# Strided attention and a Strassen MLP on one core: loads held for q instead of x, two more batches transposed by DMA, steps dealt anew

## The chip, the core and the metric

The kernel runs on one core of one Trainium2 chip. The core has five engines: TensorE (PE; its weight loads appear as PEld), VectorE (DVE), ScalarE (ACT), GpSimd (POOL) and SyncE (SP). Each works through its own list of instructions in order, and waits where an operand is not there yet. Transfers are issued by GpSimd and SyncE and carried out by 16 DMA engines. The metric is the time of one execution in microseconds; before, the median of three runs was 282.69 us (282.55 to 283.13).

## The reference

Attention over 8 batches of 8 heads (576 positions of 64), then an MLP over the 4608 tokens. Heads 0 to 3 see a local window of 32 positions, heads 4 to 7 the earlier positions with the same remainder modulo 32:

```python
rel = pos[:, None] - pos[None, :]
mask_local = (rel >= 0) & (rel < 32)
mask_strided = (rel >= 0) & (pos[None, :] % 32 == pos[:, None] % 32)
scores = np.where(masks, q @ k.T / 8, -1e9)       # masks: local for h < 4, else strided
attn = softmax(scores) @ v                        # [8, 8, 576, 64]
x = attn.transpose(0, 2, 1, 3).reshape(4608, 512)
h = x @ w_in                                      # 512 x 2048
out = (h * np.tanh(softplus(h))) @ w_out          # 2048 x 512
```

## The kernel before

Inputs are float32; GpSimd's DMAs cast them to bf16 while they load. Products are bf16 with float32 sums.

*Attention.* A batch is loaded as six tiles: `ks`, `qs` (strided k and q), `kl`, `ql` (local), `vraw` and `vl` (v for the two kinds). k and q must be transposed so that the 64 elements of a head lie along the partitions. For batches 0 to 2 TensorE transposes them, from batch 3 on four DMA transposes do, which SyncE issues: `kTs`, `qTs`, `kTl`, `qTl` (`transpose_by_dma`, L189). There is one buffer of each, so the loads of the next batch may only start once the tiles have been read. Scores, exponential (ScalarE), mask (VectorE), the product with v (L299), and the division by the sum (`norm`, L311 and L316) give `x_l` and `x_s`, the attention of the local and the strided heads, with positions on the partitions.

*From x to xT.* The MLP needs x with its 512 channels on the partitions: `xT`, a ring of four batches, 128 channels by four, where channels 0 and 1 are the local heads and 2 and 3 the strided ones. The local ones go by two DMA transposes from batch 2 on (`xt_dma`, L323). The strided ones of batches 0 to 5 are transposed by TensorE (`xt`, L346), two groups of eight matmuls a batch, each followed by a copy into `xT`. Those of batches 6 and 7 are transposed by one DMA into `ks` (`xs_dma`, L329), which is free then, and copied to `xT` in two pieces (`xs_copy`).

*MLP.* The tokens are nine blocks of 512, `t` = 0 to 8. For each, `x @ w_in`, mish (ScalarE writes `gT`), and `@ w_out`. Each product is a Strassen-Winograd product: seven products of halves instead of eight, for which VectorE makes sums of x (`xs`), of g (`gs`), of the weights (`wis`, `wos`), and of the results (`hh`, `ee`, `osb`). TensorE writes into eight PSUM banks (`set`, `ee`, `at`). Two stores of a block are issued by SyncE (L567).

*The order of the work.* Nothing is scheduled automatically. Every instruction stands where the table `PLANS` puts it: ten strings, one for each block and a last one for the rest. A function `do` reads a string word by word and emits each step's instructions to their engines. Plan `t` holds the MLP of block `t` and mostly the attention of batch `t + 1`; `^` and `_` ahead of a word mean the next or the previous `t`, `@3` names the batch. Of the words, `ld` is a load, `D:ks` a DMA transpose of k or q, `T` and `t` their transposes by TensorE and the copy, `q`, `e`, `k`, `v`, `r` scores, exponential, mask, product with v and division, `y` the two DMA transposes of local x, `X` and `xc` the transposes of strided x by TensorE and the copy, `V` and `vc` the same by DMA, `x` a sum of x, `g` and `n` sums of g, a figure the product of that number of the first layer, `m` with a figure one of the second, `st` a store. The letter behind a last colon is the engine (`D` VectorE, `A` ScalarE) or the bank.

*Holds.* GpSimd would issue loads as early as buffers allow. At seven places the table has `hold`: a copy of two elements on GpSimd out of the tile that some DMA transpose writes. GpSimd waits there until that transfer has landed, and the loads behind it on GpSimd start only then:

```python
elif f == "hold":
    e = (b % RING) * S + S - 1
    src = {"ks": kTs, "qs": qTs, "kl": kTl, "ql": qTl}[x[0]][0:1, 0:2] if x else xT[0:1, 0:2, e]
    Po.tensor_copy(hold[0:1, 0:2], src)
```

With no argument it reads `xT` (the landing of the transposed local x of batch `b`), with `qs` it reads `qTs`. Six holds of the kernel before are of the first kind, one, for the loads of batch 5, is of the second.

Of the kernel before, what the change touches and what calls it, by code (L numbers as in the profile page):

```python
# [19 lines left out]
SU = 80  # L20
CS, PN = 8, 72
# [24 lines left out]
def kernel(ctx, tc, q, k, v, moe_w_in, moe_w_out, out):  # L46
    nc = tc.nc
    B, H, S, D = q.shape
# [45 lines left out]
    x_s = sb([128, CS * 4, D], "x_s")  # L94

# [129 lines left out]
    class Attn:  # L225
# [102 lines left out]
        def xs_dma(self):  # L328
            nc.sync.dma_start_transpose(  # L329
                flat(ks)[:, 0:16 * SU].rearrange("c (u n) -> c u n", u=16),  # L330
                x_s[0:SU].rearrange("p u d -> p (u d)"),
            )

        def xs_copy(self, hf, eng):
            t0 = (self.b % RING) * S
            cast(
                eng, xT[:, 2 + hf, t0:t0 + S].rearrange("p (n j) -> p n j", j=CS),
                flat(ks)[:, 8 * SU * hf:8 * SU * hf + 8 * SU].rearrange("p (j n) -> p n j", j=CS)[:, 0:PN, :],
            )
# [229 lines left out]
    with tc.manual_schedule():  # L569
# [158 lines left out]
        def go(plan, t=0):  # L728
            for w in plan.split():
# [27 lines left out]
            ),  # L757
            (
# [6 lines left out]
            ),  # L765
            (
# [10 lines left out]
            ),  # L777
            (
# [8 lines left out]
            ),  # L787
            (
# [39 lines left out]
            ),  # L828
            (
                "m1:1 m1c:1:D _3:3 _E:3 m1c:0:D m5:0 m5:1 _4:3 g:1 m6:0 g:2 m6:1 _Z:3 m2:0 m5c:A m6c:1:D m7:1 m6c:0:A "  # L830
                "m7c:1 g:3 m2:1 z:b:A w:b:S m3:1 m7:0 m7c:0 m3:0 m3c m4:1 m4:0 z:0:A z:1:A st:1 w:0:S w:1:A "
            ),
        )
        for t, plan in enumerate(PLANS):
# [32 lines left out]
```

## Time and profile before

| | |
|---|---|
| median of three runs | 282.69 us (282.55 to 283.13) |
| the profiled execution | 283.62 us |
| its span, first to last instruction | 281.9 us |
| matmuls / weight loads in the program | 3235 recorded / 3241 |
| moved by DMA | 37.35 MB in 98242 packets |
| of the 16 DMA engines' time, loads on GpSimd's queue | 65.3% of the span |
| transposes and stores on SyncE's queue | 28.5% of the span |

The span is what the profile covers; the execution's own time is longer by what lies around it. The digits of the page are the busy share in tenths of 40 slices, each 281.9 / 40 = 7.05 us long. A timeline row is start, length, engine, line, operation, written and read tile, and in brackets the idle time before it with what ended that. Rows with a `q` behind the engine (SPq, POOLq) are issues of DMAs: their length is not the transfer's, which ends later with its landing. The profile after has lines shifted by one, since a line is added near the top.

### The profile page before, as it was taken

How to read it: one execution, taken by the hardware profiler on the slowest of the kernel's cores; microseconds unless marked ns; L12 is line 12 of the kernel's file. 1: busy time of each engine (PE TensorE's matmuls, PEld its weight loads, DVE VectorE, ACT ScalarE, POOL GpSimd, SP SyncE). 2: the span in 40 equal slices, each digit the busy share in tenths (PEclk: the TensorE clock that was granted, in tenths of full speed). 3: DMA queues.
4: the chain of work that ended last, by engine and by line, in shares of the span. 5: the costliest groups of instructions: out<-in, count | busy, mean ns of one | idle time of the engine just before them, and what ended most of it. 6: DMA issues, size and time to landing. Idle time of an engine off the chain costs nothing.

```text
span 281.9 us, 7629 instructions
## 1 busy us (share of the span) xinstructions
PE 273.2 (97%) x3235; PEld 226.5 (80%) x3241; DVE 225.5 (80%) x384; ACT 186.1 (66%) x288; POOL 57.6 (20%) x78
## 2 busy tenths in 40 slices
PE   8998999999999999999999999998999999999994
PEld 3657746678989888888898989886989888888883
DVE  3789878999899895999689969888889966837761
ACT  2577974799776797479757986687488217624830
POOL 8543421440027007200540027000100000000000
PEclk9999999999999999999999999999999999999999
DMA  7999999999929998999799989989644003002104
GB/s 142 191 207 203 205 189 197 146 222 92 168 46 141 120 168 169 193 112 155 203 147 100 137 228 145 116 146 155 161 136 96 10 2 149 2 3 98 53 0 149
DMA packets 98242, 37.35 MB, mean 133 GB/s; under 512 B 79800, under 2 KB 93688, under 8 KB 98208
## 3 DMA queue, kind: packets, MB, share of 16 engines
q0 software_dynamic: 57808, 18.30, 65.3%
q1 hardware_dynamic: 40112, 18.32, 28.5%
q8 instruction: 25, 0.41, 0.6%
q10 hardware_dynamic: 288, 0.25, 0.4%
q14 instruction: 9, 0.07, 0.1%
HBM read 37.05 MB, written 9.44 MB: 165 GB/s over the span
## 4 chain that ended last, share of the span: by engine, by line
PE 90%; DVE 3%; DMA 2%; ACT 2%; issue 1%; SPq 1%; DVEq 0%; ACTq 0%
PE set L121 52%; PE ee L121 21%; PE at L121 9%; PE at L299 4%; DMA qTs<-qs 2%; SPq L189 1%; PE at L346 1%; PE ee L346 1%; PE ee L202 1%; PE set L299 1%; DVE xs L115 1%; PE ee L208 0%; PE at L208 0%; DVE osb L112 0%; DVE wos L115 0%
## 5 line engine op out<-in xcount | busy, mean ns | idle before, releaser
L121 PEld LDWEIGHTS <-wis 128*128 128x128 bf16 x577 | 55.9, 99 | 10.4 <-issue 2.2
L121 PEld LDWEIGHTS <-gs 128*128 128x128 bf16 x512 | 48.9, 98 | 6.9 <-issue 0.5
L121 PEld LDWEIGHTS <-gT 128*128 128x128 bf16 x448 | 42.2, 98 | 9.4
L121 PEld LDWEIGHTS <-w_in 128*128 128x128 bf16 x436 | 40.8, 97 | 7.7 <-issue 1.2
L121 PE MATMUL set<-w_out,gT 128*128 128x256 bf16 (+1 forms) x299 | 46.1, 294 | 0.2
L121 PE MATMUL set<-xT,w_in 128*128 128x256 bf16 (+1 forms) x263 | 40.1, 275 | 1.0 <-ACT gT L450 0.8
L450 ACT ACTIVATE gT<-set 128x1024 bf16<-128x1024 f32 x32 | 32.8, 1024 | 8.8 <-PE set L121 7.2
L121 PE MATMUL set<-xs,wis 128*128 128x256 bf16 x256 | 38.4, 273 | 0.0
L110 ACT COPY set<-set 128x512 f32<-128x512 f32 x35 | 20.2, 576 | 16.0 <-PE set L121 14.8
L121 PE MATMUL set<-wos,gs 128*128 128x256 bf16 x224 | 28.0, 273 | 0.0
L115 DVE TENSOR_TENSOR hh<-set,hh 128x512 f32<-128x512 f32 x32 | 21.9, 685 | 5.4 <-PE set L121 5.1
L115 DVE TENSOR_TENSOR ee<-set,hh 128x512 f32<-128x512 f32 x32 | 22.3, 697 | 3.9 <-PE set L121 1.7
L448 ACT ACTIVATE gT<-hh 128x512 bf16<-128x512 f32 x35 | 22.0, 635 | 4.0 <-DVE hh L115 3.7
L686 POOL COPY hold<-xT 1x2 bf16<-1x2 bf16 x6 | 1.9, 317 | 106.3 <-DMA xT<-x_l 106.3
L115 DVE TENSOR_TENSOR gs<-gT,gs 128x2048 bf16<-128x2048 bf16 x16 | 19.5, 1221 | 3.6 <-ACT gT L448 1.8
L446 ACT ACTIVATE gT<-ee 128x512 bf16<-128x512 f32 x35 | 20.1, 595 | 2.0 <-PE ee L121 2.0
L121 PE MATMUL ee<-xs,wis 128*128 128x256 bf16 x140 | 20.8, 272 | 0.0
L121 PE MATMUL ee<-xT,wis 128*128 128x256 bf16 x140 | 20.8, 273 | 0.0
L110 ACT COPY hh<-ee 128x512 f32<-128x512 f32 x20 | 11.7, 585 | 12.5 <-PE ee L121 12.4
L115 DVE TENSOR_TENSOR gs<-gT 128x2048 bf16<-128x2048 bf16 x16 | 19.5, 1217 | 0.2 <-ACT gT L448 0.2
L316 DVE TENSOR_TENSOR x_s<-at,rden 72x768 bf16<-72x768 f32 (+1 forms) x22 | 18.8, 856 | 0.8
L121 PE MATMUL set<-xs,w_in 128*128 128x256 bf16 x128 | 19.2, 272 | 0.0
(145 smaller groups left out, 467.9 us busy)
## 6 DMA issues: line engine op xcount, KB each, us to landing
out_dram<-osb SPq DMA_DIRECT2D x17, 512.0 KB, 3.7
vl<-in_v_dram POOLq DMA_DIRECT2D x8, 288.0 KB, 12.3
w_out<-in_moe_w_out_dram POOLq DMA_DIRECT2D x4, 512.0 KB, 16.0
ks<-in_k_dram POOLq DMA_DIRECT2D x7, 288.0 KB, 11.6
qs<-in_q_dram POOLq DMA_DIRECT2D x7, 288.0 KB, 10.0
vraw<-in_v_dram POOLq DMA_DIRECT2D x7, 288.0 KB, 7.5
w_in<-in_moe_w_in_dram POOLq DMA_DIRECT2D x3, 512.0 KB, 14.6
kl<-in_k_dram POOLq DMA_DIRECT2D x10, 144.0 KB, 8.9
```

The source lines that it names most:

```text
L110: Sc.copy(out_, in_)
L115: eng.tensor_tensor(out=out_, in0=a, in1=b, op=op)
L121: PE.matmul(o, lhsT=lhsT, rhs=rhs, start=start, stop=stop, skip_group_check=True)
L189: nc.sync.dma_start_transpose(dst[:, 0:k * r].rearrange("c (u n) -> c u n", u=k), src[0:r].rearrange("p h x -> p (h x)" if n[1] == "s" els ...
L202: PE.transpose(tr[:, PN * u:PN * u + PN], src[0:PN, h, 128 * jj:128 * jj + 128], ident[0:PN, 0:PN])
L299: PE.matmul(po[:, e, i, :] if kind == "l" and self.apart else po[:, (n - n0) // per, (n - n0) % per, :], lhsT=pt[0:r, c0:c0 + 128], rhs=rh ...
L316: Dv.tensor_tensor(out=xo, in0=po[0:m, :, :, 0:D], in1=rd.unsqueeze(3).to_broadcast([m, nb, per, D]), op=ALU.mult,)
L346: PE.transpose(tr[:, n * j:n * j + n], x[0:n, u:u + 2, :].rearrange("p u d -> p (u d)"), ident[0:n, 0:n],)
L446: Sc.activation(o[:, 0:2, 256:512], two(E), AF.Mish)
L448: Sc.activation(o[:, 2:4, 256:512], two(h[:, 1, :]), AF.Mish)
L450: Sc.activation(o[:, :, 0:256].rearrange("p (b u) n -> p b u n", b=2), pair[:, 0:2, :].rearrange("p b (u n) -> p b u n", u=2), AF.Mish,)
L686: Po.tensor_copy(hold[0:1, 0:2], src)
```

## The change

Three edits. First, the DMA transpose of strided x gets a buffer of its own, `xst`, instead of `ks`. Second, the strided x of batches 4 and 5, too, is transposed by DMA (`V`, `vc`) and no longer by TensorE (`X`, `xc`). Third, the table is written anew: most steps stay near where they were but not where they stood, and two holds, those ahead of the strided q of batches 6 and 7, read `qTs` instead of `xT`.

```diff
@@ -92,6 +92,7 @@
     x_s = sb([128, CS * 4, D], "x_s")
+    xst = sb([128, 16 * SU], "xst")
@@ -327,7 +328,7 @@
         def xs_dma(self):
             nc.sync.dma_start_transpose(
-                flat(ks)[:, 0:16 * SU].rearrange("c (u n) -> c u n", u=16),
+                xst[:].rearrange("c (u n) -> c u n", u=16),
                 x_s[0:SU].rearrange("p u d -> p (u d)"),
             )
@@ -335,7 +336,7 @@
             cast(
                 eng, xT[:, 2 + hf, t0:t0 + S].rearrange("p (n j) -> p n j", j=CS),
-                flat(ks)[:, 8 * SU * hf:8 * SU * hf + 8 * SU].rearrange("p (j n) -> p n j", j=CS)[:, 0:PN, :],
+                xst[:, 8 * SU * hf:8 * SU * hf + 8 * SU].rearrange("p (j n) -> p n j", j=CS)[:, 0:PN, :],
             )
@@ -732,103 +733,103 @@
         PLANS = (
...
-                "7c:0 3:0 E:0 v:s0:A 6c:1 y:1 hold 4:0 st:1 k:s2:D 7:1 Z:0 r:s0:A 5:2 3:1 ld:vs@5 1:2 1c:2:A 7c:1 4:1 "
...
-                "7:2 7c:2 2:3 st:0 6:3 5c:3:A 6c:3 X:0:a 4:2 3:2 xc:0:a:D H:1 H:2 7:3 3:3 7c:3 ld:ks@6 Z:2 ^m1:0 E:2 n "
...
+                "hold:qs@5 st:1 ld:vs@5 ld:qs@6 H:3 "
...
+                "g:1 m5:0 g:2 _Z:3 ae q:l1:F q:l0:A m2:1 m6:1 m6:0 m6c:D e:l1:F g:3 e:l0:A k:l0:D _V q:l2:A e:l2:A "
...
```

What the table does to the order is seen engine by engine. GpSimd, from the hold behind the loads of batch 5 on to that behind the loads of batch 6; before:

```order
49 L686 COPY hold<-xT 1x2
50 L157 DMA vraw<-in_v_dram 72x4x512
51 L133 DMA qs<-in_q_dram 72x4x512
52 L151 DMA kl<-in_k_dram 96x12x64 x2
53 L151 DMA ql<-in_q_dram 96x12x64 x2
54 L133 DMA ks<-in_k_dram 72x4x512
55 L160 DMA vl_79<-in_v_dram 96x24x64
56 L686 COPY hold<-xT 1x2
```

The same place in the changed kernel:

```order
49 L687 COPY hold<-qTs 1x2
50 L158 DMA vraw<-in_v_dram 72x4x512
51 L134 DMA qs<-in_q_dram 72x4x512
52 L152 DMA kl<-in_k_dram 96x12x64 x2
53 L152 DMA ql<-in_q_dram 96x12x64 x2
54 L134 DMA ks<-in_k_dram 72x4x512
55 L161 DMA vl_79<-in_v_dram 96x24x64
56 L687 COPY hold<-qTs 1x2
```

The order is the same; rows 49 and 56 read another tile. SyncE, from the transpose of the strided q of batch 5 to the transposes of batch 6; before:

```order
18 L189 DMA_TRANSPOSE qTs<-qs 128x16x80
19 L323 DMA_TRANSPOSE xT<-x_l 128x6x96 x2
20 L567 DMA out_dram<-osb 128x2x512 x2
21 L189 DMA_TRANSPOSE kTs<-ks 128x16x80
22 L189 DMA_TRANSPOSE qTl<-ql 128x12x96
```

Changed:

```order
18 L190 DMA_TRANSPOSE qTs<-qs 128x16x80
19 L324 DMA_TRANSPOSE xT<-x_l 128x6x96 x2
20 L568 DMA out_dram<-osb 128x2x512
21 L330 DMA_TRANSPOSE xst<-x_s 128x16x80
22 L568 DMA out_dram<-osb 128x2x512
23 L190 DMA_TRANSPOSE kTs<-ks 128x16x80
24 L190 DMA_TRANSPOSE qTl<-ql 128x12x96
```

A transpose of x_s (of batch 4 here, and of batch 5 one round on) has come between the two stores. VectorE, where the attention of batch 2 is divided by its sums (`rden`) into `x_l`; before:

```order
118 L112 COPY set_102<-set_102 128x512
119 L311 RECIPROCAL rden<-at 96x2x6
120 L316 TENSOR_TENSOR x_l<-at,rden 96x768
121 L115 TENSOR_TENSOR gs<-gT,gs 128x2048
122 L311 RECIPROCAL rden<-at 96x2x6
123 L316 TENSOR_TENSOR x_l<-at,rden 96x768
```

Changed:

```order
118 L312 RECIPROCAL rden<-at 96x2x6
119 L317 TENSOR_TENSOR x_l<-at,rden 96x768
120 L113 COPY set_103<-set_103 128x512
121 L312 RECIPROCAL rden<-at 96x2x6
122 L317 TENSOR_TENSOR x_l<-at,rden 96x768
123 L116 TENSOR_TENSOR gs<-gT,gs 128x2048
```

The second `x_l` row now stands ahead of the `gs` sum instead of behind it. In all, TensorE has 3209 matmuls and weight loads instead of 3241, VectorE 369 rows instead of 377, ScalarE 297 instead of 289.

More of the change, by code (lines that the diff above doesn't have):

```diff
@@ L734 @@
                 "ld:ks@0 ld:qs@0 ld:vs@0 clear:1 clear:0 kc:D un:1:a un:1:a un:1:a un:1:a un:1:a un:1:a un:1:a un:1:a "
[22 rows of a table removed]
-            ),
-            (
[6 rows of a table removed]
-            ),
-            (
[10 rows of a table removed]
-            ),
-            (
[8 rows of a table removed]
-            ),
-            (
[8 rows of a table removed]
-            ),
-            (
[7 rows of a table removed]
-            ),
-            (
[7 rows of a table removed]
-            ),
-            (
[5 rows of a table removed]
-            ),
-            (
[4 rows of a table removed]
-            ),
-            (
-                "m1:1 m1c:1:D _3:3 _E:3 m1c:0:D m5:0 m5:1 _4:3 g:1 m6:0 g:2 m6:1 _Z:3 m2:0 m5c:A m6c:1:D m7:1 m6c:0:A "
-                "m7c:1 g:3 m2:1 z:b:A w:b:S m3:1 m7:0 m7c:0 m3:0 m3c m4:1 m4:0 z:0:A z:1:A st:1 w:0:S w:1:A "
[21 rows of a table added]
+            ),
+            (
[7 rows of a table added]
+            ),
+            (
[9 rows of a table added]
+            ),
+            (
[8 rows of a table added]
+            ),
+            (
[7 rows of a table added]
+            ),
+            (
[8 rows of a table added]
+            ),
+            (
[7 rows of a table added]
+            ),
+            (
[5 rows of a table added]
+            ),
+            (
[5 rows of a table added]
+            ),
+            (
+                "g:1 m5:0 _4:3 m1c:1:D m5:1 m5c:A m1c:0:D m6:0 m6c:0:A m3:1 g:2 m6:1 m7:0 m7c:0 _Z:3 g:3 m2:1 m6c:1:A "
+                "m2:0 m7:1 m7c:1 m3:0 m3c m4:1 z:b:A m4:0 w:b:S st:1 z:0:A z:1:A w:0:S w:1:A "
             ),
```

150 rows, old and new, of the table PLANS are left out of this document.

## The prediction

> **What bounds the kernel now.** I read the page first (share of each engine, then the chain that ended last), then the timeline of TensorE for the places where it stands still, then the timelines of the two queues that feed it, SyncE and GpSimd. A timeline row begins with start and length; in brackets stands the idle time before it and what ended that.
>
> ```profile
> span 281.9 us, 7629 instructions
> PE 273.2 (97%) x3235; PEld 226.5 (80%) x3241; DVE 225.5 (80%) x384; ACT 186.1 (66%) x288; POOL 57.6 (20%) x78
> DMA  7999999999929998999799989989644003002104
> PE 90%; DVE 3%; DMA 2%; ACT 2%; issue 1%; SPq 1%; DVEq 0%; ACTq 0%
> ```
>
> TensorE works through the whole span and is nine tenths of the chain. But the DMA row is as full as TensorE up to slice 28 (about 200 us) and then nearly empty: until then two resources run side by side, each about as long as the other. Where they meet shows in the timeline of TensorE and in the chain around 188 us.
>
> ```profile
> 113.23 1.91 PE L121 MATMUL set<-w_out,gs 128*128 128x256 bf16 x16 [0.55 <-DVE osb L115]
> 136.10 0.20 PE L121 MATMUL set<-qTs,kTs 64*128 64x72 bf16 x1
> 165.60 0.20 PE L121 MATMUL set<-qTs,kTs 64*128 64x72 bf16 x1
> 188.12 5.85 DMA qTs<-qs
> 194.10 0.19 PE L121 MATMUL set<-qTs,kTs 64*128 64x72 bf16 x1 [1.28 <-DMA qTs<-qs]
> ```
>
> The last row is the first strided score product of batch 7. It waits 1.28 us for the transposed strided q, which lands at 188.12 + 5.85 = 193.97. In batches 5 and 6 the same product starts at 136.10 and 165.60 without a wait. So I follow how the transposed q of each batch comes about. The rows of SyncE (SP) are the issue of each DMA, those of GpSimd (POOL) the `hold` copies, whose end lets the next batch's loads start.
>
> ```profile
> 73.75 2.04 SPq L189 DMA_TRANSPOSE qTs<-qs  x1
> 78.44 2.51 SPq L323 DMA_TRANSPOSE xT<-x_l  x2
> 82.42 0.47 POOL L686 COPY hold<-xT 1x2 bf16<-1x2 bf16 x1 [23.05 <-DMA xT<-x_l]
> 97.29 1.30 SPq L189 DMA_TRANSPOSE kTl<-kl  x1
> 106.78 0.17 POOL L686 COPY hold<-qTs 1x2 bf16<-1x2 bf16 x1 [16.79 <-DMA qTs<-qs]
> 124.86 1.33 SPq L189 DMA_TRANSPOSE kTs<-ks  x1
> 130.46 1.80 SPq L189 DMA_TRANSPOSE qTs<-qs  x1
> 136.99 0.18 POOL L686 COPY hold<-xT 1x2 bf16<-1x2 bf16 x1 [22.52 <-DMA xT<-x_l]
> 154.13 1.34 SPq L189 DMA_TRANSPOSE kTs<-ks  x1
> 159.28 2.52 SPq L189 DMA_TRANSPOSE qTs<-qs  x1
> 166.69 0.17 POOL L686 COPY hold<-xT 1x2 bf16<-1x2 bf16 x1 [22.24 <-DMA xT<-x_l]
> 182.48 2.45 SPq L189 DMA_TRANSPOSE kTs<-ks  x1
> qTs<-qs SPq DMA_TRANSPOSE x5, 4.7
> ```
>
> It is a ring: hold, loads, four transposes, transposes of the output x, hold. With the median landing time of 4.7 us, qTs of batch 5 lands at about 135.2 and that of batch 6 at 164.0. From batch 5 to batch 7 that is 58.8 us for two rounds. TensorE's own rounds are 165.60 - 136.10 = 29.5 us. DMA and TensorE keep step, and batch 7 shows DMA falling behind. The forecast is therefore a sum along this ring up to the product at 194.10; what stands behind that product has the same TensorE work before and after.
>
> **The change part by part.** (a) *Loads held less.* The rows of GpSimd shown with the change: the instructions and their order stay, two holds, those at 136.99 and 166.69 of now, read another tile. The hold at 106.78 already is of the new kind and prices it: from the landing of q to the next `kTs` issue, which waits for `ks`, it took 124.86 - 106.78 = 18.1 us. With the late hold it took 154.13 - 135.2 = 18.9 and 182.48 - 164.0 = 18.5. So lifting the hold gains about 0.6 us a round, not the 2 us by which the copy itself moves, because the transposes of x and the stores still have to go through the same DMA engines. Two rounds: **-1.2 us**. Bounds: 0 (against 18.1, the shorter late round is only 0.4 longer) to -1.6.
>
> (b) *Strided x of batches 4 and 5 by DMA.* By the rows of SyncE shown with the change, one more transpose stands between the two stores of each round. Batch 7 already has such a transpose, late, with nothing beside it. The windows view gives its DMA work (stretch, length, busy time of each engine, clock, DMA share, GB/s):
>
> ```profile
> 215.82 1.35 SPq L329 DMA_TRANSPOSE ks<-x_s  x1
> 216.00:220.00 4.00, 4.00 (x39) 3.60 (x37) 3.32 (x4) 2.90 (x5) 0.00 (x0) 1.00 0.47 82
> 164.40:169.20 4.80, 4.80 (x76) 3.90 (x74) 3.37 (x7) 3.60 (x8) 2.10 (x4) 1.00 0.82 263
> ```
>
> 0.47 x 4.0 = 1.9 us of all 16 engines. What 1.9 us cost the loads beside them, I take from (a): the loads of batch 4 had DMA to themselves and took 97.29 - 82.42 = 14.9 us to the first transpose; those of batch 5, with two transposes of x and two stores beside them, 18.1. Those four transfers are 0.82 x 4.8 = 3.9 us of work (third row), so a microsecond beside the loads cost 3.2 / 3.9 = 0.82. Price: 1.9 x 0.82 = 1.5 us a round, **+3.0 us** for two. Bounds: 0 (it fits into idle DMA) and 1.9 each.
>
> [...]
>
> (c) *Transposed x of batch 2 earlier.* Its second `x_l` row on VectorE (DVE), with whose end SP issues the two `xT<-x_l` of 78.44, moves ahead of a `gs` sum (the rows of VectorE shown with the change).
>
> ```profile
> 76.36 0.53 PE L299 MATMUL at<-vl,Pl 128*128 128x65 bf16 x12
> 77.45 0.95 DVE L316 TENSOR_TENSOR x_l<-at,rden 96x768 bf16<-96x768 f32 x1
> 104.84 1.05 PE L121 MATMUL set<-w_out,gT 128*128 128x256 bf16 x8
> 105.72 1.04 PE L121 MATMUL set<-wos,gs 128*128 128x256 bf16 x8
> ```
>
> The value products of 76.36 also move, ahead of two groups of eight w_out products; two neighbouring groups start 0.88 us apart (last two rows). So they end at 76.36 - 1.76 + 0.53 = 75.1; with reciprocal and product (1.2 us) x stands at about 76.4 instead of 78.40. SP is free then (73.75 + 2.04 = 75.79). The hold comes at about 80.4, 2.0 earlier, and the ring starts that much earlier: **-2.0 us**. It cannot be much more, as qTs of batch 3 lands only at 73.75 + 4.7 = 78.45; little less either, since no step of TensorE that the ring waits for follows until batch 7.
>
> (d) *The last four transposes.* In batch 7 they take 193.97 - 182.48 = 11.5 us, in batches 5 and 6 135.2 - 124.86 = 10.3 and 164.0 - 154.13 = 9.9; the first issue alone is 2.45 against 1.33 and 1.34. Nothing in the program makes batch 7 longer, so I put in the mean of the three, 10.6: **-0.9 us** (bounds 0 and -1.6).
>
> (e) *TensorE and the copies.* 32 transposes fall away, in four groups of eight:
>
> ```profile
> 156.12 0.42 PE L346 MATMUL at<-consts_sb,x_s 72*128 72x72 bf16 x8
> 156.38 0.60 PE L121 MATMUL set<-xs,w_in 128*128 128x256 bf16 x4
> 195.21 0.72 DVE L112 COPY xT<-ks 128x576 bf16<-128x576 bf16 x1 [1.07 <-DMA ks<-x_s]
> ```
>
> A group holds TensorE for 0.26 us, so 1.0 us in all. The stall of 0.55 at 113.23 should go too, as the `gs` sum that VectorE did before that `osb` row moves ahead. Against this, score products stand apart from each other at two more places, which I put at 0.4 us. Together -1.2 us, but all of it ahead of the product at 194.10, which waits for DMA anyway: it counts **0** in this sum and is the floor of rival B. The copies into xT stay two a batch (0.72 each, third row); eight other copies go from VectorE (80% busy) to ScalarE (66%), also ahead of that wait. The new wait is that for `xst`. Behind its copy on VectorE stand the sums of x that the first `xs` products need. In batch 4 the transpose is issued about 136.1 by today's clock (behind one store), lands like the one before 195.21 some 5.2 us later, and with copy and sum the products may start at 142.5. Between the score product of 136.10 and them now stand eight groups at 0.88 and some 1.5 us of smaller ones, so TensorE comes at 144.6: hidden, with 2 us to spare; in batch 5, with seven groups, 1 us.
>
> **Sum.** -2.0 - 1.2 + 3.0 - 0.9 + 0 = -1.1 us: the product of 194.10 starts at 193.0, the span becomes 280.8. The profiled execution took 283.62 us, 1.7 around its span; the median of the three runs shown is 282.69, so the forecast is 282.69 - 1.1 = **281.6 us**.
>
> **The rivals.** *B, TensorE sets the end.* The two transposes fit into idle DMA (bound 0 in (b)); then q of batch 7 is there in time, and TensorE gains its wait of 1.28 and the 1.2 of (e): -2.4, **280.3**. For it speaks that a hold lifted early leaves loads to fill gaps; against it that DMA is at 9 tenths in every slice there. *C, slower: the transposes cost in full.* If each delays the loads by 1.9 us and the early hold gains nothing, (a) and (b) are +3.8 instead of +1.8; with the -2.0 of (c) and batch 7 at 11.5 again, q of batch 7 lands 1.8 us late: **284.5**. It decides from the point where the two rounds cost over 2 us more than now. Its mark in this trace is 0.82 per us, near 1. [...] *D, no net change.* The lead of (c) and the gain of (a) pay for the two transposes, batch 7 keeps its 11.5 us: -2.0 - 1.2 + 3.0 = -0.2, **282.5**.
>
> **How the numbers follow.** Chances: forecast 40% (alone 281.0 to 282.3), B 18%, C 22%, D 20%. What a measurement of this kernel can tell from no change is about 0.2%, 0.57 us. Faster: 30 of the 40, all 18 of B, 2 of D: 50%. Same: 10 of the forecast, 15 of D: 25%. Slower: C and 3 of D: 25%. The range runs from B without the 0.4 that (e) charges, 279.9, to 284.2, which leaves out the worse half of C.
>
> **What would show it.** Right: the copy for batch 4's loads ends near 80.4; a round from one `kTs` issue to the next is about 30 us (29.3 and 28.4 now); the first strided score product of batch 7 still waits for `qTs<-qs`, at about 193. Each term falls apart from the others: (c) if the first hold is not 2 us earlier, (a) and (b) by the time from the landing of q to the next `kTs` issue (19.6 expected). The forecast is wrong if that product waits for nothing (B), if a wait for `xst` appears on VectorE with TensorE idle behind it, or if idle time appears where steps were dealt anew: the start before 60 us, where I count no change, or the last 80 us.

## The result and the profile after

The changed kernel is slower. Its median over six runs is 290.96 us (287.81 to 293.42), against 282.91 us (282.35 to 283.46) for six runs of the kernel before; the ratio is 1.0263 with a 95% interval of 1.021 to 1.0316. An execution over 1.5% longer than the fastest of its kernel counts as slow (one of the changed kernel's six does), and the ratios, like the medians given for the experiments, leave such executions out. The forecast was 281.6 us, the range 279.9 to 284.2. The profiled execution took 291.15 us.

From the page of the changed kernel: span, busy time of each engine, granted clock and DMA by slices, and the chain that ended last, by engine.

```profile
span 289.4 us, 7580 instructions
PE 274.6 (95%) x3209; PEld 225.9 (78%) x3209; DVE 219.6 (76%) x376; ACT 190.7 (66%) x296; POOL 58.0 (20%) x78
PE   8899999999999999999919999999999999999994
PEclk9999999999999999999977999999999999999999
DMA  7999999999959799998999999966523303003004
PE 80%; DMA 11%; DVE 3%; ACT 3%; issue 1%; POOL 1%; DVEq 0%; ACTq 0%; POOLq 0%
```

Slice 21 (145 to 152 us) stands out: TensorE is nearly empty there, and in slices 21 and 22 the granted clock falls to 0.7. DMA's share of the chain has grown from 2% to 11%. TensorE's timeline names the place; its first row is the first `xs` product of block 4, the second that of block 5, the last the first strided score product of batch 7.

```profile
152.36 1.01 PE L122 MATMUL ee<-xs,wis 128*128 128x256 bf16 x4 [6.89 <-DVE xs L116]
182.64 0.60 PE L122 MATMUL ee<-xs,wis 128*128 128x256 bf16 x4 [0.41 <-DVE xs L116]
201.89 0.20 PE L122 MATMUL set<-qTs,kTs 64*128 64x72 bf16 x1
```

TensorE waits 6.89 us for the sums of x, and these wait on VectorE for the new transpose, as VectorE's timeline shows:

```profile
150.54 0.72 DVE L113 COPY xT<-xst 128x576 bf16<-128x576 bf16 x1 [8.37 <-DMA xst<-x_s]
151.17 0.68 DVE L113 COPY vs<-vraw 72x2048 bf16<-72x2048 bf16 x1
151.88 0.42 DVE L116 TENSOR_TENSOR xs<-xT 128x512 bf16<-128x512 bf16 x1
```

In the chain of waits the two transposes of strided x are the long pieces (start, length until landing):

```profile
136.48 14.04 DMA xst<-x_s
170.61 9.85 DMA xst<-x_s
```

14.04 and 9.85 us, where I had put 5.2. What runs beside them is seen on the queues. GpSimd's holds (the first row still reads `xT`, the others `qTs`) end where the loads start; SyncE's timeline has the issues around the first transpose.

```profile
81.22 0.17 POOL L687 COPY hold<-xT 1x2 bf16<-1x2 bf16 x1 [20.98 <-DMA xT<-x_l]
106.65 0.17 POOL L687 COPY hold<-qTs 1x2 bf16<-1x2 bf16 x1 [18.01 <-DMA qTs<-qs]
135.12 0.60 POOL L687 COPY hold<-qTs 1x2 bf16<-1x2 bf16 x1 [20.97 <-DMA qTs<-qs]
165.33 1.22 POOL L687 COPY hold<-qTs 1x2 bf16<-1x2 bf16 x1 [22.78 <-DMA qTs<-qs]
```

```profile
132.41 3.35 SPq L324 DMA_TRANSPOSE xT<-x_l  x2
135.81 0.57 SPq L568 DMA_DIRECT2D out_dram<-osb  x1
136.48 5.05 SPq L330 DMA_TRANSPOSE xst<-x_s  x1
141.63 0.69 SPq L568 DMA_DIRECT2D out_dram<-osb  x1
155.49 1.33 SPq L190 DMA_TRANSPOSE kTs<-ks  x1
...
184.29 1.33 SPq L190 DMA_TRANSPOSE kTs<-ks  x1
```

The loads are let in at 135.1 and 165.3, the transposes of x are issued behind that, at 136.5 and 170.6. The issue alone holds SyncE for 5.05 us, where the like one of batch 7 took 1.35 before. Then the stall takes its toll a second time, in the windows view (stretch, length, busy time of each engine, granted clock, DMA share, GB/s):

```profile
140.00:145.00 5.00, 5.00 (x57) 4.50 (x55) 2.09 (x4) 1.25 (x4) 2.55 (x3) 1.00 1.42 108
149.00:152.00 3.00, 0.00 (x0) 0.00 (x0) 1.43 (x3) 1.46 (x2) 0.00 (x0) 0.50 1.94 223
152.50:155.00 2.50, 2.50 (x15) 1.80 (x14) 1.87 (x4) 0.84 (x2) 0.00 (x0) 0.50 2.10 173
155.50:158.00 2.50, 2.50 (x37) 2.27 (x35) 2.25 (x5) 2.07 (x3) 0.00 (x0) 1.00 1.16 134
```

When TensorE starts again its clock is granted at half, until about 155.5: 3.1 us of work at half speed are 1.55 us lost. The difference of the spans, 289.4 - 281.9 = 7.5 us, adds up nearly: 6.89 and 0.41 of stalls, 1.55 of half clock, 0.9 by which the start is later in this execution (the first strided score product of batch 2 at 56.00 against 55.09), less 1.6 for two waits of before that shrank (1.28 and 0.55 to 0 and 0.25) and 1.0 for the 32 matmuls that are gone: 7.2.

### The profile page after: what moved, and what is told of

It is laid out like the page before. It is cut to its first block, busy times and chain, and to the rows that moved or that the text cites. A ratio compares the mean times of both kernels' runs of the same rounds, so it can differ in the third digit from the quotient of the medians.

```text
span 289.4 us, 7580 instructions
## 1 busy us (share of the span) xinstructions
PE 274.6 (95%) x3209; PEld 225.9 (78%) x3209; DVE 219.6 (76%) x376; ACT 190.7 (66%) x296; POOL 58.0 (20%) x78
## 3 DMA queue, kind: packets, MB, share of 16 engines
q0 software_dynamic: 57808, 18.30, 61.5%
## 4 chain that ended last, share of the span: by engine, by line
PE 80%; DMA 11%; DVE 3%; ACT 3%; issue 1%; POOL 1%; DVEq 0%; ACTq 0%; POOLq 0%
PE set L122 48%; PE ee L122 18%; DMA xst<-x_s 8%; PE at L122 7%; PE at L300 4%; DMA kl<-in_k_dram 3%; PE ee L209 1%; ACT Pl L272 1%; PE ee L347 1%; ACT osb L111 0%; DVE ee L116 0%; DVE hh L116 0%; PE set L300 0%; ACT xT L111 0%; DVE gs L116 0%
## 5 line engine op out<-in xcount | busy, mean ns | idle before, releaser
L122 PEld LDWEIGHTS <-w_in 128*128 128x128 bf16 x436 | 41.6, 98 | 7.1 <-issue 0.4
L111 ACT COPY hh<-ee 128x512 f32<-128x512 f32 x30 | 17.6, 587 | 11.6 <-PE ee L122 11.5
L111 ACT COPY set<-set 128x512 f32<-128x512 f32 x30 | 17.5, 582 | 10.6 <-PE set L122 10.6
L449 ACT ACTIVATE gT<-hh 128x512 bf16<-128x512 f32 x35 | 21.4, 630 | 4.4 <-DVE hh L116 4.3
L447 ACT ACTIVATE gT<-ee 128x512 bf16<-128x512 f32 x35 | 20.4, 595 | 4.0 <-PE ee L122 4.0
L122 PE MATMUL ee<-wos,gT 128*128 128x256 bf16 x128 | 16.5, 273 | 0.0
```

The lines of the kernel that those rows point to most:

```text
L111: Sc.copy(out_, in_)
L122: PE.matmul(o, lhsT=lhsT, rhs=rhs, start=start, stop=stop, skip_group_check=True)
L447: Sc.activation(o[:, 0:2, 256:512], two(E), AF.Mish)
L449: Sc.activation(o[:, 2:4, 256:512], two(h[:, 1, :]), AF.Mish)
```

## The experiments

The theory after this profile, called "loads": the transpose of strided x is slow because the early hold lets six loads into the DMA engines ahead of it. Its rivals: the stores beside it on SyncE are to blame ("store"), or the steps dealt anew are slow by themselves ("table"). The edits are in the words of the table.

**1. Without the loads.** The six loads behind the first early hold are left out.

```diff
- hold:qs@5 st:1 ld:vs@5 ld:qs@6 H:3
+ hold:qs@5 st:1 H:3
- ... _ld:kl@6 _ld:ql@6 ... _ld:ks@6 ... ld:vl@6 ...
```

> The changed kernel without the six loads behind the first early hold (v of batch 5; q, k and local v of batch 6); these tiles keep the data of the batch before. Theory 'loads': in the changed kernel the transpose of batch 4's strided x is issued at 136.5 and lands at 150.5, 14.0 us later, because the early hold lets these loads in at 135.1, ahead of it. Without them it should land within 4 to 6 us and TensorE's stall of 6.89 us at 152.36 should be gone (under 0.5). Rival 'store': the two 512 KB stores beside it on SyncE slow it; then it still takes over 9 us and the stall stays over 2 us.

One run: 282.34 us. The stall is gone. In VectorE's timeline the copy waits 0.17 us for a transpose that was issued at 137.16:

```profile
142.72 0.72 DVE L113 COPY xT<-xst 128x576 bf16<-128x576 bf16 x1 [0.17 <-DMA xst<-x_s]
```

So it lands 5.5 us behind its issue, within the 4 to 6 expected, with both stores still there. It is the loads that slow the transpose; the time itself is not comparable, as this kernel moves less.

**2. Both stores behind the transpose**, in both rounds.

```diff
- hold:qs@5 st:1 ld:vs@5 ...  k:l0:D _V q:l2:A
+ hold:qs@5 ld:vs@5 ...  k:l0:D _V _st:1 q:l2:A
```

> The changed kernel with the first store of both rounds issued behind the transpose of strided x instead of ahead of it; the loads stay. Theory 'loads': the transpose is issued 0.7 us earlier and still takes over 10 us; the stall of TensorE at batch 4 stays between 5 and 7 us, the time within 1.5 us of the changed kernel. Rival 'store': the transpose takes 4 to 6 us, and the stall falls below 1 us.

One run: 288.35 us. Neither guess held in full: the chain has the transpose with 10.62 us, as "loads" had it, but TensorE's stall falls to 2.98, between the two.

```profile
135.38 10.62 DMA xst<-x_s
```

**3. Strided x by TensorE again**, with table and early holds of the change (the division of batch 5's strided x moves ahead with its transposes).

```diff
- ... _V ... vc:1:D@4 ... vc:0:A@4 ... _V ... vc:0:A@5 ... vc:1:D@5
+ ... X:0:a X:1:A xc:0:a:D xc:1:A:D ... X:0:a ... xc:0:a:D X:1:A ... _xc:1:A:D
```

> The changed kernel with the strided x of batches 4 and 5 transposed by TensorE again (32 matmuls and four copies back, the two DMA transposes and their copies gone); table and early holds stay. If the wait for the transposes is all that made the change slower, no stall over 1 us remains near batches 4 and 5, the granted clock stays at 1.00, and the time is 281 to 284 us: about 1 us of matmuls more than the changed kernel, 7.3 us of stalls and about 1.7 us of half clock less. Rival 'table': the steps dealt anew are slow by themselves; then it stays above 285.

285.18 us, ratio 1.0083 (1.0058 to 1.0107). The large stalls and the half clock are gone (the mean granted clock is 1.00), some 6 of the 8 us, but it is slower than expected and, by some 2.4 us, than before. Its stalls, 2.1 us, stand at places where I had put the transposes back (0.44, 0.23 and 1.45 us, the largest a transpose that waits for the bank of the one before it). But the profile of before has 1.8 us of stalls (1.28 and 0.55) that are gone here, so most of the 2.4 us has no cause found, and "table" is not excluded as the cause of up to 2 us.

**4. Holds on the transposed local x again**, as before the change.

```diff
- hold:qs@5 st:1 ...  hold:qs@6 k:s2:D
+ hold st:1 ...  hold k:s2:D
```

> The changed kernel with the two holds reading the transposed local x again, as before the change; the DMA transposes of strided x stay. Theory 'loads': the loads start about 2 us later (137.3 instead of 135.1), behind the issue of the transpose of strided x, which should then land 6 to 9 us after its issue instead of 14.0; TensorE's stall at batch 4 falls from 6.89 to 0 to 2.5 us, and the time to 282 to 286 us. If the transpose is slow whatever is released when, the stall stays over 5 us and the time within 1 us of 291.

288.77 us, ratio 1.0218 (1.0172 to 1.0263). The first half held: the transpose is issued at 135.06 and its first copy runs at 140.45 without a wait; the stall of 6.89 falls to 1.20. The time did not follow, because two other tiles are late now. VectorE's timeline:

```profile
144.37 0.69 DVE L113 COPY vs<-vraw 72x2048 bf16<-72x2048 bf16 x1 [2.66 <-DMA vraw<-in_v_dram]
...
197.12 0.72 DVE L113 COPY xT<-xst 128x576 bf16<-128x576 bf16 x1 [5.18 <-DMA xst<-x_s]
```

The first is the spread of v, which stands ahead of the sums of x; by this hold its load starts 1.5 us later, counted from the hold before (29.99 us behind it, against 28.47 in the changed kernel). The second is the copy of batch 6's strided x, ahead of two masks on which TensorE then waits 3.77 us. In the changed kernel both were covered by the large stall.

**5. The transpose of strided x first**, then local x, then both stores; early holds.

```diff
- y:0 y:1 r:s2:A ... _V q:l2:A
+ r:s2:A V y:0 y:1 ... q:l2:A
```

> The changed kernel with the transpose of strided x issued ahead of the two of local x, and both stores behind these, in both rounds; the early holds stay. Theory 'loads': in the round of batch 4 it is issued at about 132, over 2 us before the loads are released, lands in 4 to 6 us, and the wait for it is gone; what stands behind it on SyncE now runs beside the loads, so the local x lands at 139 to 142 instead of 137.1, still ahead of the sums at 144. No stall over 1 us near 145, time 282 to 285 us. Against it: if what is behind the transpose now lands after 144, the stall stays, only with another tile named.

290.64 us, ratio 1.0278 (1.0236 to 1.0319): the expectation was wrong, and what it named as speaking against it came true in another place. The strided x landed in 4.7 us, as expected; now local x is behind it, beside the loads (chain of waits, then VectorE's timeline):

```profile
137.18 9.18 DMA xT<-x_l
```

```profile
146.48 0.95 DVE L317 TENSOR_TENSOR x_l<-at,rden 96x768 bf16<-96x768 f32 x1 [4.66 <-DMA xT<-x_l]
```

Batch 5 wants to write `x_l`, of which there is one, while the transfer of batch 4's still reads it. In the chains of the changed kernel and of experiments 2 and 5, what SyncE issues behind the release of the loads takes 9 to 14 us; which transfer is put there decides who waits.

**6. The early holds in the kernel before**, and nothing else.

```diff
- y:1 hold 4:0 st:1 ...  y:1 hold 4:0 st:1
+ y:1 hold:qs@5 4:0 st:1 ...  y:1 hold:qs@6 4:0 st:1
```

> The kernel before with nothing changed but the two holds, which read the transposed strided q as in the change. By the ring of the prediction the loads gain about 0.6 us a round, q of batch 7 lands 1.2 us earlier, TensorE's wait of 1.28 us before batch 7 falls to about 0.1, and the time is 0.3 to 1.2 us below before (ratio 0.996 to 0.999). Theory 'loads' adds: the stores issued beside the earlier loads take 6 to 10 us instead of 3 to 4, which costs nothing as long as nobody waits for them. If the early hold by itself does harm, the ratio is over 1.002.

282.36 us against 282.70 for before in the same job, ratio 0.9987 (0.9975 to 0.9999): as expected, and of the kernels that do all the work the only one not slower than before, though by no more than a measurement can just tell. GpSimd's holds, SyncE's `kTs` issues and TensorE's first strided score product of batch 7:

```profile
135.28 0.31 POOL L686 COPY hold<-qTs 1x2 bf16<-1x2 bf16 x1 [20.39 <-DMA qTs<-qs]
163.31 0.51 POOL L686 COPY hold<-qTs 1x2 bf16<-1x2 bf16 x1 [20.58 <-DMA qTs<-qs]
```

```profile
152.98 1.34 SPq L189 DMA_TRANSPOSE kTs<-ks  x1
...
181.56 2.44 SPq L189 DMA_TRANSPOSE kTs<-ks  x1
```

```profile
193.13 0.20 PE L121 MATMUL set<-qTs,kTs 64*128 64x72 bf16 x1
```

From the landing of q, with which the hold now ends, to the `kTs` issue it takes 17.7 and 18.25 us, where the late holds had 18.9 and 18.5: 1.45 us gained, most of it in the first round, and the wait for q is gone. Behind the release stand the two stores of each round, for which nobody waits; they take 6.9 us (median) in the first round and 3.2 in the second, where 6 to 10 were expected.

**7. Without the two stores** around the transpose of batch 4.

```diff
- hold:qs@5 st:1 ld:vs@5 ...  _ld:ql@6 _st:0 k:s0:D
+ hold:qs@5 ld:vs@5 ...  _ld:ql@6 k:s0:D
```

> The changed kernel without the two stores around the transpose of batch 4's strided x (this block's output is left out); loads and early holds stay. If the loads alone slow the transpose, it still takes 9 us or more from its issue; if the store ahead had its share, as the second experiment hints (10.6 us with both stores behind it, 14.0 with one ahead), it takes 6 to 9 us and the stall at batch 4 is under 2.5 us.

One run: 291.89 us. The chain:

```profile
135.69 10.76 DMA xst<-x_s
```

Without any store it takes as long as with both behind it (10.62). The loads alone make the 5.5 us of experiment 1 into 10.76, as the theory had it. That the time is no better than the changed kernel's has another reason in this profile: behind a stall of 3.18 us TensorE works for 5.7 us at half clock (148.29 to 154.0), and from 181.95 on for another 2.7 us, in which groups of four products take 1.01, 0.85 and 0.85 us, and 0.44 later.

**8. Holds on the transposed strided x**, in both rounds. The loads start behind its landing; the first round:

```diff
- hold:qs@5 ... ld:vs@5 ld:qs@6 ...  _V q:l2:A
+ ... _V _hold:x _ld:vs@5 _ld:qs@6 q:l2:A
```

> The changed kernel with both holds reading the transposed strided x itself, so that the loads start behind its landing. Theory 'loads': the transposes land in 4 to 6 us and the first stall is gone; but the loads of batch 6 start at about 141 instead of 135, and by the ring the transposed q of batches 6 and 7 comes 3 to 6 us later than in the changed kernel: new waits of 2 to 7 us in all before the first strided scores of batches 6 and 7, time 284 to 290 us. If the loads had slack, no wait appears there and the time is 281 to 283.

One run: 286.31 us. With no load beside it, only the two stores, the transpose needs 4.30 us (chain), a third of the 14.04:

```profile
135.24 4.30 DMA xst<-x_s
140.25 5.38 DMA vraw<-in_v_dram
```

The waits came elsewhere than expected: none for q, but again the spread of v, whose load now starts at 140.25, holds VectorE for 3.74 us and TensorE for 2.15.

**9. The change mended.** Late holds, the spread of v behind the sums of x, and batch 6's copies behind the masks.

```diff
- hold:qs@5 st:1 ...  m3:0 sp:D vc:0:A@4 ...  v:l1:A x:2 5c:0:A
+ hold st:1 ...  m3:0 vc:0:A@4 ...  v:l1:A x:2 sp:D 5c:0:A
- g:2 e:l1:F vc:0:D@6 ...  sh:D vc:1:D@6 m3:0 x:0 x:1 m2:1 k:l1:D k:l0:D x:3
+ g:2 e:l1:F ...  sh:D k:l1:D k:l0:D vc:0:D@6 vc:1:D@6 m3:0 x:0 x:1 m2:1 x:3
```

> The changed kernel with three things moved: both holds read the transposed local x again (as in the fourth experiment); on VectorE the spread of v (vs<-vraw), which there waited until 144.37 ahead of the first sums of x, stands behind them; and the copies of batch 6's transposed strided x, on which VectorE waited until 197.12 ahead of two masks, stand behind these masks. If these are the waits that the late loads left, both stalls (1.20 and 3.77 us) and the half clock go, and the span falls from 286.7 to 280.0 to 282.0, the time to 281.7 to 283.7. If the table is slow for another reason, it stays above 284.5.

283.58 us, ratio 1.0049 (1.002 to 1.0078). 5 us of the fourth kernel's 288.77 are won back by moving three steps on VectorE; both stalls are gone. What is left in the profile (of an execution of 287.27 us, 3.7 above the median, so its size is not typical) is a wait at the ring of the prediction, in TensorE's timeline:

```profile
193.95 0.51 PE L122 MATMUL at<-qTl,kTl 64*128 64x96 bf16 x8 [2.67 <-DMA qTl<-ql]
```

Whether the 0.5% that are left are the price of the two transposes in the ring or of the steps dealt anew is not shown: experiment 3, without the two transposes, is 0.8% slower than before.

**10. The ninth kernel with the start of before.**

```diff
+ _ld:ql@3 v:l0:A@2 r:l0:A@2 _H:3 m5:1 m1c:D _E:3 _ld:qs@3 sh:D@3 D:ql@3 D:kl@3 m2:0 v:l1:A@2 _Z:3 m2:1
- D:ql@3 D:kl@3 v:l1:A@2 m5:1 m1c:D _Z:3 m2:0 m2:1
```

> The ninth kernel with the first two strings of the table (the start and block 1) taken from the kernel before, the rest as there. The first score product of batch 2 stands at 55.09 before and at 56.00 in the changed kernel; if the start dealt anew costs these 0.9 us, this one is 0.5 to 1.2 us faster than the ninth kernel, 280.8 to 283.0, and at least as fast as before. If later waits take the lead back, the two agree within 0.3 us.

285.87 us, ratio 1.0109 (1.0082 to 1.0137). The time tells nothing of the start: where the two tables are joined TensorE stands still for 1.1, 0.4 and 0.6 us between 77 and 82, and one product of block 1 (`m2:0`) there reads part of `gT` before its last mish is written. The profiles answer the question: by the changed table's start the first strided score product of batch 2 comes at 55.20 to 56.63 in eleven profiles, by that of before at 55.09, at 55.76 (experiment 6) and, in this kernel, at 56.37. The 0.9 us lie within what executions differ by; no cost of the start is shown.

**11 and 12. The second kernel and the change, timed side by side.** Edit 11 is edit 2.

> The second kernel (both stores behind the transpose of strided x, loads and early holds as in the change) timed in five rounds, beside the changed kernel on the same chip. One look gave 288.35 us with the transpose taking 10.6 us, where the changed kernel had 14.0. If the store ahead of the transpose costs these 3 us, this kernel is 1.5 to 4 us faster than the changed one here. If the 14.0 was the luck of one execution, the two agree within 1 us, at 288 to 291.

> The changed kernel itself, as the standard for the run beside it: 290 to 291 us, and in its profile again a wait of VectorE of 4 to 9 us for the transpose of batch 4's strided x, issued beside the loads. If the profile shows that transpose landing within 6 us of its issue, the first profile was no standard.

288.32 us (ratio 1.0185, 1.014 to 1.0229) and 289.37 us (1.023, 1.0174 to 1.0287). The two are 1.05 us apart, less than the 1.5 to 4 expected, and their intervals overlap: that the store ahead costs time is not shown. On the transpose of batch 4 it weighs in two profiles each: 14.04 and 13.00 us with the store ahead, 10.62 and 10.5 with both behind. In 11 TensorE waits 2.60 us for the sums of x; then the long piece of the chain is a store, which frees its buffer late, and TensorE waits another 1.15 us for the copy behind that. In 12 (an execution of 293.83 us, 4.5 above the median) it is the transposes again. Chains, of 11 first:

```profile
137.11 11.67 DMA out_dram<-osb
```

```profile
135.78 13.00 DMA xst<-x_s
169.99 11.92 DMA xst<-x_s
```

The change again has 13.0 and 11.9 us for its transposes; the issue of the first held SyncE for 4.67 us, against 1.63 in kernel 11. With the store ahead but no load, in experiments 1 and 8, the issue took 1.68 and 1.67. So in the round of batch 4 store and loads together hold up the issue. The round of batch 5 does not show it: there the issue took 2.5 to 2.8 us in the change and in experiments 2, 11 and 12, with the store ahead or behind.

## Why the prediction was wrong

**The failed step is the last price of (e)**: the transpose of strided x "lands like the one before 195.21 some 5.2 us later", hidden with 2 us to spare. That row stood in a stretch without loads; part (a) of the same change puts six loads beside it. In the changed kernel it took 14.04 and 9.85 us, without loads 5.5, with loads held until its landing 4.30. 14.04 - 5.2 = 8.8 us more, less the 2 us to spare: 6.8, and the stall is 6.89. That this fits so closely is in part luck: TensorE came at 145.5 instead of 144.6, but the transpose was issued 0.4 us later than put in, and from its landing to the first `xs` product it took 1.8 us instead of 1.2, because the spread of v (the `vs` row) stands between. In (b) I worked out what the transpose costs the loads and never what the loads cost the transpose. The half clock behind the stall, 1.55 us, had no price either.

**(a) the early hold: right for the ring.** Forecast -1.2 us for two rounds; experiment 6 alone gives 1.45 there, but a time only 0.34 us lower. The wait of 1.28 us that goes with it stood in a profile 0.9 us above the median of before, so it may be shorter in most executions; no run tells.

**(b) the two transposes in the ring: right for the sum of the two rounds.** From hold to the next `kTs` issue I expected 19.6 us; it took 155.49 - 135.12 = 20.4 and 184.29 - 165.33 = 19.0. Against the 17.7 and 18.25 of experiment 6, which has the early holds without the transposes, that is 3.4 us for both where 3.0 were forecast; in experiments 2 and 11 the rounds took 20.0 to 21.0, so the price may be higher.

**(c) x of batch 2 earlier: half right.** The hold ended 1.2 us earlier (81.22 against 82.42), not 2.0; at the next hold 0.1 was left (106.65 against 106.78). That stretch is 25.4 us long here and 24.5 to 25.4 in the eleven profiles of the changed table, against 24.4 before and 24.3 in experiment 6. So part of the loss is this execution's and part is not; "little less either" was wrong.

**(d) the last four transposes: right in direction.** By the trace they took 9.1 us, less than the 10.6 put in. All in all q of batch 7 landed at 193.4, and the ring had forecast 192.9. That the sum along the ring was good to half a microsecond is luck: (c) brought 1.9 us too little and (d) 1.5 too much. And it no longer set the end, as TensorE came to that product at 201.89.

**The rivals.** None is what happened. C had the sign, but counted the delay for the loads only; its 284.5 is 6.5 us below what was measured. That a wait for `xst` could appear with TensorE idle behind it stood in the prediction as a sign of failure, without a price and without a share of the chances. That was the missing rival.

**What stays open**: the last 2 us of experiment 3, and why the transpose takes two to three times as long beside the loads (9.85 to 14.04 us against 4.30 and 5.5); no run separates the loads' number from their small packets (GpSimd's queue moves 18.30 MB in 57808 packets, 317 bytes each on average). Sharing alone does not explain it: from 144 to 145 us in the changed kernel the DMA engines moved 7 GB/s, at a share of 0.07, while the transpose was still under way.

## What to carry to other kernels

When a change moves a release and adds a transfer, price each with the other in place: a duration from a quiet stretch need not hold where the stretch does not stay quiet (here 5.2 us, and 14.04 beside six loads). A hold that looks like lost time may be what keeps a short transfer on the critical path ahead of long ones (the transpose of strided x took 4.30 us with the loads held until its landing); here it could be lifted at no cost where only stores stand behind it (experiment 6, ratio 0.9987). And on an engine that works in order, ask of every late tile what stands behind its reader: in experiments 4, 5 and 8 each cure exposed the next wait, and three steps moved on VectorE won back 5 us.

## What the runs showed of the hardware

Behind some short stalls TensorE worked for some microseconds at half clock, behind others it did not. Windows of experiment 8 around its stall of 2.15 us, then of experiment 5 around one of 2.95 us:

```profile
144.60:146.60 2.00, 0.00 (x0) 0.00 (x0) 0.95 (x2) 0.15 (x1) 2.00 (x4) 1.00 1.26 163
147.00:150.00 3.00, 3.00 (x25) 2.33 (x24) 1.77 (x4) 1.05 (x2) 0.76 (x1) 0.50 2.39 157
150.50:153.00 2.50, 2.50 (x34) 2.28 (x32) 2.50 (x5) 2.30 (x3) 0.00 (x0) 1.00 2.33 164
```

```profile
146.20:149.00 2.80, 0.00 (x0) 0.00 (x0) 2.51 (x4) 0.64 (x1) 0.00 (x0) 1.00 1.22 331
149.10:152.00 2.90, 2.90 (x36) 2.51 (x36) 2.87 (x6) 2.02 (x5) 0.00 (x0) 1.00 2.35 162
```

The shorter stall was followed by over 3 us at half clock (0.50 from 147 to 150). The longer one was followed by none (1.00 from 149.1 to 152); those of 1.20 (experiment 4) and 1.45 us (experiment 3) were not either, the granted clock stayed at 1.00 there. In experiments 7 and 12 TensorE works at half speed for 2.7 us behind the wait for batch 5's strided x, for which VectorE stands still for 2.75 and 2.72 us: in both chains groups of four products take 1.01, 0.85 and 0.85 us there (from 181.95 and 184.09 on) and 0.44 later. What decides between these cases no run shows.
